# A hand-written instruction order replaced: step 0's queries are loaded first, W_in's four pieces in a row, and 118 steps sit on another engine

## The chip, the cores and the metric

The kernel runs on one NeuronCore of a Trainium2 chip. The core has TensorE (PE, matmuls and transposes into PSUM), VectorE (DVE), ScalarE (ACT), GpSimd (POOL) and SyncE (SP, which here only issues DMAs). Each engine works through its own instructions strictly in the order in which they were written, and waits at an instruction until everything that it reads or overwrites is ready. The metric is the time of one launch on the device, in microseconds (us). The kernel before takes 145.53 us, the median of three runs (145.13 to 146.61).

## The reference

A decayed linear attention (4 batches, 8 heads, 768 positions, head size 64, blocks of 64) is followed by a gated MLP with a spatial mixing matrix over the 768 positions. Inputs and output are float32.

```python
for b in range(nb):                                  # attention, block by block
    intra = einsum('bhic,bhjc->bhij', qb, kb) * Dmask
    intra = einsum('bhij,bhjd->bhid', intra, vb)
    inter = einsum('bhid,bhde->bhie', qb * lam_pow, kv_state)
    out[:, :, sl] = intra + inter
    kv_state = lam_block * kv_state + einsum('bhsd,bhse->bhde', kb * rev_pow, vb)
...
h = maximum(x @ w_in, 0); u, v = split(h)             # 512 -> 1024, halves of 512
v_n = (v - mean(v)) / sqrt(var(v) + 1e-06)
v_s = einsum('ts,bsd->btd', w_spatial, v_n) + b_spatial
return (u * v_s) @ w_out
```

## The kernel before, in words

Each batch of 768 positions is cut into three steps of 256, so the program has steps n = 0 to 11; batch b owns steps 3b to 3b+2. Attention and the first matrix product go step by step. The spatial mixing needs all three steps of a batch and so comes once a batch, and the output product follows it.

The whole order of the work is a string, ORDER, of 719 tokens such as `PV.0.1.6.T`. A token names a step of the work, its arguments (for most: the step or batch, a half or a part, at the end the PSUM bank or banks) and the engine: T is PE, D is DVE, A is ACT, P is POOL, S a DMA on SP's queue. The kernel emits the tokens from first to last under a manual schedule, so that each engine's instruction stream is the subsequence of its own letters. Data dependences, and the reuse of a buffer or of a bank, become semaphore waits. Eight PSUM banks exist, of which bank 7 holds the running state.

The steps that the text speaks of, with the lines of the profile:

- Loads (L196): LK.n, LQ.n, LV.n bring a step's keys, queries and values, 512 KB each, into three buffers per kind (n mod 3). WH.0 to WH.3 (L253) bring W_in in four pieces of 512 KB: 0 and 1 hold the v columns, 2 and 3 the u columns. WQ.0 to WQ.5 (L274) bring 128 rows each of W_spatial; WQ.0 and WQ.1 land where WH.0 and WH.1 were, WQ.4 and WQ.5 where WH.2 and WH.3 were, WQ.2 and WQ.3 in a place of their own. WP (L283) brings W_out, 1 MB.
- Casts to bf16 (L181 on ACT, L183 on DVE, L185 on POOL): CW.0 to CW.3 for W_in's v columns (512 elements a partition), CX.0 and CX.1 for its u columns (1024), WC.a for W_spatial (768), WX.0 and WX.1 for W_out (1024), VC.n or the halves VD.n for the values.
- Attention: KM and QM (L331) scale keys and queries by powers of lambda; TK and TQ (L366) transpose them on PE and EK and EQ copy them out of PSUM, in steps 0 to 6, where steps 7 to 11 use DMA transposes instead, DK (L344) and DQ (L348). SC (L396) makes the scores, MK (L401) masks them on DVE, KP (L425) adds to the state, SX, SY and SA (L440) copy the state out, AV (L459 for the state's part, L468 for the values) forms the output in two halves, EX (L486, shown at L181 or L183) puts it into SBUF as x transposed. FN is a read of one element that orders AV's two halves.
- MLP: PV (L493) makes v for 128 positions, EV (L498 on ACT, L500 on DVE) applies the maximum, BN (L508, L509) takes mean and variance, RA, RD and RB (L513, L518, L523) turn them into scale and shift, VN (L529 on ACT, L532 on DVE) normalizes. PU (L544) makes half of u for a step and EU (L498, L500) evicts it.
- Mixing: WT (L556) transposes W_spatial on PE and EW copies it out. GP (shown at L181 or L183) writes the bias into a bank, PW (L570, six matmuls of 384 columns) adds the mixing to it, GM (L576) multiplies by u. The last two matmuls of every PW read the normalized v of the third step of its batch, so that no PW ends before the last VN of its batch.
- Output: PO (L581) and PH (L590), EO and EH (copies), ST and SH (stores).
- Fillers: FL (L309) multiplies a tile of ones into a bank that nobody reads. There are 32 such matmuls, in both versions.

Of the kernel before, what the change touches and what calls it, by code (L numbers as in the profile page):

```python
# [36 lines left out]
GM.0.1.0.5.D GM.0.2.0.6.D WT.2.1.3.T WT.0.1.1.T EW.0.1.1.D WP.S VC.3.D EW.2.1.3.A GP.0.1.1.6.A PW.0.3.0.2.T
WT.1.1.4.T LK.5.S GM.0.3.0.2.D SC.3.1.0.1.T KP.3.5.T SC.3.0.2.3.T MK.3.1.0.1.D EW.1.1.4.A PW.0.1.1.6.T TK.4.2.0.T
MK.3.0.2.3.D GP.0.3.1.1.A GP.0.2.1.2.A SY.3.5.A PW.0.3.1.1.T SA.3.1.D SX.3.D GM.0.1.1.6.D GP.0.0.1.3.A TQ.4.2.4.T
PW.0.2.1.2.T GM.0.2.1.2.D GM.0.3.1.1.D PW.0.0.1.3.T GM.0.0.1.3.D EK.4.2.0.A EQ.4.2.4.A KM.5.0.P KM.5.1.P  # L40
AV.3.0.5.6.T SC.4.0.1.2.T KP.4.0.T FN.3.5.6.A AV.3.1.5.6.T SY.4.0.D SC.4.1.3.4.T EX.3.1.6.A TQ.5.2.0.T WX.0.A WX.1.A
EX.3.0.5.D MK.4.0.1.2.D SA.4.1.D MK.4.1.3.4.D SA.4.0.D LV.5.S PV.3.1.6.T PU.3.1.5.T PO.0.1.1.T PO.0.3.2.T TK.5.2.4.T
PV.3.0.3.T LV.6.S LK.6.S EK.5.2.4.D EO.0.1.1.A EQ.5.2.0.A EV.3.1.6.A EU.3.1.5.A EO.0.3.2.D VC.5.P AV.4.0.6.0.T
KP.5.6.T SC.5.0.1.2.T EV.3.0.3.A FN.4.6.0.D SC.5.1.4.5.T AV.4.1.6.0.T PU.3.0.3.T VC.6.P SA.5.0.D MK.5.1.4.5.D
MK.5.0.1.2.D KM.6.0.P KM.6.1.P LK.7.S LQ.7.S LQ.6.S KM.7.1.P QM.7.0.P QM.6.0.P QM.6.1.P EX.4.1.0.A EX.4.0.6.A
PV.4.1.0.T PV.4.0.4.T AV.5.0.1.5.T BN.3.1.D FN.5.1.5.D KP.6.2.T AV.5.1.1.5.T EV.4.0.4.A PO.0.2.4.T PO.0.0.6.T
# [597 lines left out]
```

## Time and profile before

| what | value |
|---|---|
| median of three runs | 145.53 us (145.13 to 146.61) |
| the profiled execution's own time | 144.71 us |
| its span, first to last instruction | 143.0 us |
| mean granted PE clock | 0.972 of full speed |
| busy: PE, DVE, ACT, POOL | 94%, 81%, 58%, 36% of the span |
| read from and written to HBM | 24.38 MB and 6.29 MB |

The span is the part that the trace shows; 1.7 us of the execution's own time lie around it. The 40-slice view has one digit for each 3.6 us: a 9 is an engine that is busy throughout. The busy time of PE contains the time in which a matmul waits in the array's pipeline, so that a full digit does not by itself mean full speed; the chain of waits tells which of its pieces released the next. In the rows of that chain the columns are the start in us, the length in us, and engine, tile, line and count.

### The profile page before, as it was taken

How to read it: one execution, taken by the hardware profiler on the slowest of the kernel's cores; microseconds unless marked ns; L12 is line 12 of the kernel's file. 1: busy time of each engine (PE TensorE's matmuls, PEld its weight loads, DVE VectorE, ACT ScalarE, POOL GpSimd, SP SyncE). 2: the span in 40 equal slices, each digit the busy share in tenths (PEclk: the TensorE clock that was granted, in tenths of full speed). 3: DMA queues.
4: the chain of work that ended last, by engine and by line, in shares of the span. 5: the costliest groups of instructions: out<-in, count | busy, mean ns of one | idle time of the engine just before them, and what ended most of it. 6: DMA issues, size and time to landing. Idle time of an engine off the chain costs nothing.

```text
span 143.0 us, 4741 instructions
## 1 busy us (share of the span) xinstructions
PE 133.8 (94%) x1999; PEld 87.7 (61%) x2014; DVE 115.3 (81%) x236; ACT 82.8 (58%) x158; POOL 51.9 (36%) x61
## 2 busy tenths in 40 slices
PE   5969999899999899999999999999999999999990
PEld 4448774676666667567666565676665665666630
DVE  3399798989997769699399988995798889874760
ACT  3422895798978577569611586689113627791121
POOL 5077710555095343991770006920822000000000
PEclk9975899999999999999999999999999999999998
DMA  3999999899999899959904799998994403930284
GB/s 87 347 347 346 386 323 315 294 339 313 337 302 344 259 288 324 285 166 290 293 0 78 49 282 354 180 142 238 276 257 126 177 5 117 406 139 0 78 324 185
DMA packets 54617, 33.60 MB, mean 235 GB/s; under 512 B 11715, under 2 KB 49859, under 8 KB 54596
## 3 DMA queue, kind: packets, MB, share of 16 engines
q1 hardware_dynamic: 54448, 33.17, 80.7%
q8 instruction: 15, 0.25, 0.7%
q10 hardware_dynamic: 148, 0.13, 0.3%
q14 instruction: 6, 0.05, 0.1%
HBM read 24.38 MB, written 6.29 MB: 215 GB/s over the span
## 4 chain that ended last, share of the span: by engine, by line
PE 83%; DVE 9%; ACT 3%; issue 2%; DVEq 0%; ACTq 0%
PE ps L570 21%; PE ps L581 14%; PE ps L493 13%; PE ps L544 11%; PE ps L396 5%; PE ps L366 5%; PE ps L309 4%; PE ps L468 4%; PE ps L425 3%; PE ps L459 2%; DVE st L508 2%; DVE qc L331 2%; DVE kc L331 2%; DVE vn L532 1%; DVE win_sb L183 1%
## 5 line engine op out<-in xcount | busy, mean ns | idle before, releaser
L570 PE MATMUL ps<-wt_sb,vn 128*128 128x384 bf16 x192 | 33.7, 326 | 0.5 <-ACT vn L529 0.3
L331 POOL TENSOR_TENSOR kc<-k_in,lv 128x512 bf16<-128x512 f32 x20 | 20.5, 1043 | 30.0 <-PE ps L493 11.5
L401 DVE TENSOR_TENSOR a_sb<-ps,m 128x1024 bf16<-128x1024 f32 x24 | 28.4, 1211 | 0.7 <-PE ps L425 0.6
L570 PEld LDWEIGHTS <-vn 128*128 128x128 bf16 x192 | 18.3, 98 | 12.3 <-ACT vn L529 0.6
L544 PE MATMUL ps<-xT,win_sb 128*128 128x256 bf16 x192 | 23.6, 273 | 0.5 <-DVE win_sb L183 0.5
L331 POOL TENSOR_TENSOR qc<-q_in,lqn 128x512 bf16<-128x512 f32 x18 | 19.3, 1090 | 10.2 <-DMA q_in<-in_q_dram 5.2
L493 PE MATMUL ps<-win_sb,xT 128*128 128x512 bf16 x89 | 22.3, 379 | 0.4
L581 PE MATMUL ps<-wout_sb,gT 128*128 128x512 bf16 x84 | 22.1, 379 | 0.4
L576 DVE TENSOR_TENSOR gT<-ps,uT 128x384 bf16<-128x384 f32 x32 | 16.8, 551 | 7.1 <-PE ps L570 6.7
L544 PEld LDWEIGHTS <-win_sb 128*128 128x128 bf16 x192 | 18.4, 98 | 5.1 <-DVE win_sb L183 0.7
L181 ACT ACTIVATE ps<-bsp 128x384 f32<-128x384 f32 x23 | 11.2, 490 | 10.7 <-DVE gT L576 6.7
L508 DVE BATCH_NORM_STATS2 st<-vh 128x6 f32<-128x512 bf16 x24 | 16.2, 676 | 1.1 <-ACT vh L498 1.1
L181 ACT ACTIVATE o_sb<-ps 128x512 f32<-128x512 f32 (+1 forms) x14 | 8.0, 579 | 15.4 <-PE ps L581 14.6
L493 PEld LDWEIGHTS <-xT 128*128 128x128 bf16 x96 | 8.8, 98 | 9.6 <-ACT xT L181 0.8
L498 ACT ACTIVATE vh<-ps 128x512 bf16<-128x512 f32 x20 | 11.7, 600 | 4.9 <-PE ps L493 3.2
L181 ACT ACTIVATE xT<-ps 128x512 bf16<-128x512 f32 x20 | 11.0, 598 | 5.8 <-PE ps L468 5.7
L581 PEld LDWEIGHTS <-gT 128*128 128x128 bf16 x92 | 8.7, 98 | 8.6
L498 ACT ACTIVATE uT<-ps 128x512 bf16<-128x512 f32 x20 | 11.7, 590 | 2.0 <-PE ps L544 2.0
L468 PE MATMUL ps<-a_sb,vb 64*64 64x128 bf16 x384 | 10.2, 220 | 0.3 <-issue 0.3
L396 PE MATMUL ps<-qT,kT 64*64 64x128 bf16 x384 | 9.7, 226 | 0.0
L309 PE MATMUL ps<-ones 128*128 128x256 bf16 x32 | 7.5, 368 | 1.6 <-DVE ones L305 1.5
L185 POOL CAST vb<-v_in 128x1024 bf16<-128x1024 f32 (+1 forms) x6 | 5.8, 965 | 7.8 <-PE ps L468 7.8
(79 smaller groups left out, 175.1 us busy)
## 6 DMA issues: line engine op xcount, KB each, us to landing
k_in<-in_k_dram SPq DMA_DIRECT2D x12, 512.0 KB, 6.4
q_in<-in_q_dram SPq DMA_DIRECT2D x12, 512.0 KB, 5.9
v_in<-in_v_dram SPq DMA_DIRECT2D x12, 512.0 KB, 6.1
out_dram<-o_sb SPq DMA_DIRECT2D x23, 256.0 KB, 2.5
wst<-in_moe_w_in_dram SPq DMA_DIRECT2D x4, 512.0 KB, 7.8
wst<-in_moe_w_spatial_dram SPq DMA_DIRECT2D x4, 384.0 KB, 4.5
wst<-in_moe_w_out_dram SPq DMA_DIRECT2D x1, 1024.0 KB, 8.9
wss<-in_moe_w_spatial_dram SPq DMA_DIRECT2D x2, 384.0 KB, 7.7
```

The lines of the kernel that those rows point to most:

```text
L181: nc.scalar.activation(out=o, in_=i, func=AF.Copy)
L331: vec(e).tensor_tensor(out=dst[n % NCA][:, u].rearrange("p u m o d -> p o (u m) d"), in0=src[n % NIN].rearrange("p (o u) m d -> p o u m d" ...
L396: nc.tensor.matmul(out=pa[o][row(c), w, j], lhsT=kT[n % NTR][row(o), u, j, c * Q64:(c + 1) * Q64], rhs=qv(n, o, u, c), start=(w == 0 and j ...
L401: nc.vector.tensor_tensor(out=a_sb[n % NA][:, i].rearrange("p o w j x -> p o w (j x)"), in0=ps[:, b0:b1 + 1:b1 - b0].rearrange("p o (w y) ...
L468: nc.tensor.matmul(out=po[c ^ o][row(w), c, i], lhsT=vb[n % NCA][row(c), 4 * o + u, j, :], rhs=a[row(c), i, o, w, j, :], start=(r == 0 and ...
L493: nc.tensor.matmul(out=bank(b), lhsT=x[:, slot(c, g)], rhs=win_sb[:, g, DH:DFF], start=(g == 0), stop=(g == NCH - 1))
L498: nc.scalar.activation(out=o, in_=i, func=AF.Relu)
L508: nc.vector.bn_stats(out=st6[p2][:, t], in_=vh[p2][:, t])
L544: nc.tensor.matmul(out=pu[:, f2].rearrange("p (c x) -> p c x", c=2), lhsT=win_sb[:, g, f * P:(f + 1) * P], rhs=x[:, slot(0, g):slot(1, g) ...
L570: nc.tensor.matmul(out=bank(b)[:, 0:HW], lhsT=vn[bb % 2][:, s, f * P:(f + 1) * P], rhs=wt_sb[:, s, i * HW:(i + 1) * HW], start=False, stop ...
L576: nc.vector.tensor_tensor(out=gT[bb % 2][:, f, cols], in0=bank(b)[:, 0:HW], in1=uT[bb % 2][:, f, cols], op=ALU.mult)
L581: nc.tensor.matmul(out=bank(b), lhsT=gT[bb % 2][:, f, t * P:(t + 1) * P], rhs=wout_sb[:, f, :], start=(f == 0), stop=(f == NCH - 1))
```

## The change

Nothing but the string ORDER is changed. The two strings hold the same 719 steps (the same 32 fillers among them); they stand in another order, many use other PSUM banks, and 118 of them name another engine. On each engine:

- Moved between engines, counted over the program: EO eight from ACT to DVE and seven back; EU six from ACT to DVE and three back; EV six and three; GP four and seven; VN two from ACT to DVE and five back; EX two and four; QM six from DVE to POOL and six back; KM two and four; VC three from ACT to POOL, two from POOL to ACT, one from DVE to ACT.
- In the part of batch 0 alone: CW.0 and CW.1 go from ACT to POOL, CW.2 from POOL and CW.3 from ACT to DVE; CX.0 from POOL and CX.1 from DVE to ACT; WC.0 and WC.1 from POOL to DVE, WC.3 from DVE and WC.4 from ACT to POOL, WC.5 from DVE to ACT; both QM.3 from DVE to POOL; EW.0.0 and EW.2.0 from ACT to DVE and EW.1.0 from DVE to ACT; EV.2.0 and EU.0.1 from ACT to DVE; EU.1.0, GP.0.2.0 and VC.3 from DVE to ACT; WX.0 from ACT to POOL and WX.1 from ACT to DVE.
- SP's queue, first part. Before: K0 Q0 Q1 K1 V0 Q2 K2 V1 WH.0 WH.1 V2 Q3 WH.3 WQ.0 WQ.1 WQ.2 WH.2 K3 K4 WQ.3 WQ.4 WQ.5 V3 Q4 Q5 V4 WP K5 V5. After: Q0 K0 K1 V0 Q1 K2 Q2 V1 WH.0 WH.1 WH.2 WH.3 V2 WQ.2 WQ.1 WQ.0 K3 WQ.3 WQ.4 WQ.5 Q3 V3 Q4 K4 V4 WP Q5 K5 V5.
- PE, first part: 24 of the 32 fillers stand ahead of the first transpose (14 before); the six PV and six PU of batch 0 and the first half of W_spatial's transposes come ahead of the first PW in both versions. TQ.3 stands ahead of the first PW before, TK.3 in its place after. The first two bias writes, GP.0.2.0 and GP.0.3.0, stand in ACT's stream ahead of the evictions of step 2; before, the first ones stand behind the last EU and VN of batch 0.
- Later: the four PU that separate the last PV of batch 2 from its first PW are 8.0, 6.1, 8.1 and 6.0, with no PO between them (before: three PU, PO.1.1 and PU.8.0).

The diff, cut to the lines of the first 37 us and to one place in each of batches 0 and 2 further on:

```diff
-LK.0.S LQ.0.S LQ.1.S LK.1.S LV.0.S LQ.2.S BR.A lam.A tab.0.A msk.P idn.P posk.P one.D row.D FL.2.256.0.1.T
...
-LV.1.S WH.0.S WH.1.S LV.2.S LQ.3.S WH.3.S VD.1.1.P CW.2.P EQ.1.0.1.D SX.0.D EQ.1.1.5.A SY.0.2.A EK.1.1.3.A
...
-EK.2.0.3.A SC.2.1.4.5.T FL.1.256.6.1.T CW.0.A CW.1.A SC.2.0.2.3.T AV.1.1.0.1.T WQ.0.S WQ.1.S WQ.2.S WH.2.S WC.0.P
-WC.1.P WC.2.P MK.2.1.4.5.D MK.2.0.2.3.D SA.1.1.D VC.2.D CW.3.A EX.1.1.1.A EX.1.0.0.A PV.0.1.6.T PV.0.0.4.T
-PV.1.0.5.T KP.2.6.T AV.2.0.2.3.T SA.2.0.D EV.0.1.6.A FN.2.2.3.A EV.0.0.4.A GP.0.0.0.1.A PV.1.1.6.T FL.1.256.0.1.T
-AV.2.1.2.3.T EX.2.0.2.A QM.3.1.D QM.3.0.D TQ.3.2.4.T CX.1.D PU.0.1.0.T PU.1.1.2.T EX.2.1.3.A EV.1.1.6.A BN.0.0.D
-EV.1.0.5.A BN.0.1.D RA.0.A EU.0.1.0.A EU.1.1.2.A PV.2.0.3.T PV.2.1.6.T BN.1.1.D BN.1.0.D EV.2.0.3.A RA.1.A
-EV.2.1.6.A WT.0.0.3.T WT.2.0.5.T EW.2.0.5.A PU.2.1.2.T WT.1.0.0.T BN.2.0.D RD.1.D BN.2.1.D VN.1.1.D RD.0.D RB.0.D
-EW.0.0.3.A RA.2.A VN.0.0.A CX.0.P PU.2.0.6.T EU.2.0.6.A VN.0.1.A EW.1.0.0.D RD.2.D LK.3.S PU.1.0.5.T PU.0.0.3.T
-VN.2.0.D VN.1.0.D VN.2.1.D LK.4.S WQ.3.S EU.1.0.5.D GP.0.2.0.6.D EU.2.1.2.A GP.0.1.0.5.A EU.0.0.3.A GP.0.3.0.2.A
...
-PU.8.1.3.T PU.6.1.4.T PU.7.0.5.T EV.8.0.2.A EU.8.1.3.A GP.2.2.0.2.A EU.6.1.4.A RA.7.A BN.8.1.D RD.6.D BN.8.0.D
...
+LQ.0.S LK.0.S LK.1.S LV.0.S LQ.1.S LK.2.S LQ.2.S LV.1.S WH.0.S WH.1.S BR.A lam.A tab.0.A posk.P idn.P msk.P one.D
...
+LN.3.A mkc.D LL.D BE.1.5.D eps.D LX.A KM.0.0.D KM.0.1.D FL.2.256.1.1.T FL.2.256.2.1.T FL.2.256.4.1.T FL.2.256.2.1.T
+FL.4.256.4.1.T FL.2.256.5.1.T QM.0.0.P FL.2.256.1.1.T TQ.0.0.0.T QM.0.1.P TK.0.1.6.T TK.0.0.3.T TQ.0.1.5.T
...
+AV.0.1.5.4.T TK.2.0.6.T FL.2.256.2.1.T FL.2.256.3.1.T TQ.2.1.2.T VD.1.1.A EX.0.0.5.A QM.2.0.P WH.2.S WH.3.S LV.2.S
+MK.1.1.0.1.D EQ.2.1.2.D FL.1.256.3.1.T KP.1.3.T AV.1.0.5.0.T TQ.2.0.1.T CW.0.P CW.1.P EX.0.1.4.A FN.1.5.0.A
+EK.2.0.6.A SA.1.0.D SY.1.3.D EQ.2.0.1.D AV.1.1.5.0.T SC.2.1.3.4.T EX.1.0.5.A EX.1.1.0.A SC.2.0.1.2.T SA.1.1.D CW.2.D
+CW.3.D PV.0.1.6.T EV.0.1.6.A CX.0.A PV.0.0.5.T PV.1.1.0.T PV.1.0.6.T EV.0.0.5.A PU.1.0.5.T MK.2.1.3.4.D BN.0.1.D
+MK.2.0.1.2.D BN.0.0.D WQ.2.S WC.2.P CX.1.A EV.1.1.0.A VC.2.D PU.0.1.2.T AV.2.0.3.4.T KP.2.6.T WQ.1.S WQ.0.S LK.3.S
+WQ.3.S WQ.4.S WQ.5.S LQ.3.S LV.3.S LQ.4.S PU.1.1.1.T KM.3.0.P KM.3.1.P WC.3.P WC.4.P GP.0.2.0.0.A EU.1.0.5.A RA.0.A
+EV.1.0.6.A GP.0.3.0.5.A FN.2.3.4.A BN.1.1.D SA.2.0.D BN.1.0.D RA.1.A RD.0.D WC.1.D RD.1.D VN.1.1.D WC.0.D RB.0.D
+VN.1.0.D EU.0.1.2.D AV.2.1.3.4.T EX.2.1.4.A EX.2.0.3.A PU.0.0.6.T PV.2.1.4.T WT.2.0.3.T EW.2.0.3.D EU.1.1.1.A
+EU.0.0.6.A EV.2.1.4.A BN.2.1.D WT.0.0.1.T PV.2.0.6.T WT.1.0.2.T PU.2.0.4.T VN.0.0.A VN.0.1.A EW.1.0.2.A EV.2.0.6.D
+BN.2.0.D PU.2.1.6.T TK.3.2.3.T EW.0.0.1.D EU.2.0.4.A RA.2.A GP.0.1.0.4.A EU.2.1.6.A WC.5.A GP.0.0.0.6.A EK.3.2.3.A
+RD.2.D VN.2.0.D VN.2.1.D PW.0.2.0.0.T PW.0.3.0.5.T WT.0.1.2.T WT.2.1.1.T PW.0.0.0.6.T LK.4.S EW.0.1.2.D GM.0.2.0.0.D
...
+SC.4.0.2.3.T AV.3.1.4.1.T EX.3.0.4.A WX.1.D PO.0.3.0.T EX.3.1.1.A PV.3.0.4.T EV.3.0.4.A KM.5.0.P MK.4.1.5.6.D
...
+RD.6.D RB.6.D VN.6.1.D BN.7.0.D EU.7.1.2.A EU.7.0.3.A EV.8.1.5.A VN.6.0.A EV.8.0.0.D BN.8.0.D BN.8.1.D PU.8.0.4.T
+PU.6.1.2.T RA.7.A RD.7.D RB.7.D GP.2.3.1.1.A RA.8.A RD.8.D VN.7.0.A VN.7.1.D RB.8.D VN.8.0.D VN.8.1.A PU.8.1.3.T
+QM.9.1.D EU.8.1.3.D PU.6.0.5.T PW.2.2.1.6.T PW.2.3.1.1.T EU.8.0.4.A GP.2.2.0.0.A GP.2.1.0.3.A PW.2.2.0.0.T
+PW.2.1.0.3.T ST.1.1.S DQ.9.S QM.10.1.P DQ.10.S DK.10.S ST.0.1.S GM.2.2.1.6.D GP.2.1.1.4.A GM.2.3.1.1.D GP.2.3.0.6.D
...
```

More of the change, by code (lines that the diff above doesn't have):

```diff
@@ L37 @@
[L37 to L46, printed above, removed]
@@ L85 @@
+GM.3.3.0.0.D GM.3.2.1.3.D GP.3.2.0.5.D GP.3.3.1.1.A PW.3.1.1.6.T GM.3.1.1.6.D PW.3.3.1.1.T GM.3.3.1.1.D PW.3.2.0.5.T
+GM.3.0.0.2.D ST.2.1.S GM.3.2.0.5.D ST.2.2.S ST.1.3.S ST.1.0.S ST.2.3.S ST.2.4.S ST.1.2.S ST.2.5.S ST.2.0.S
+PO.3.3.4.T PH.3.5.1.0.T EO.3.3.4.D PO.3.0.2.T PH.3.5.0.3.T PO.3.4.6.T PO.3.2.1.T EO.3.0.2.D EH.3.5.1.0.D
+EH.3.5.0.3.A SH.3.5.1.A PO.3.1.4.T EO.3.1.4.A ST.3.3.S ST.3.0.S SH.3.5.0.S EO.3.4.6.D ST.3.4.S EO.3.2.1.D ST.3.2.S
+ST.3.1.S
 """
```

91 lines of the change are left out of this document (44 added, 47 removed).

## Prediction

> **What bounds the kernel now.** I read the page first, for who is busy and when.
>
> ```profile
> span 143.0 us, 4741 instructions
> PE 133.8 (94%) x1999; PEld 87.7 (61%) x2014; DVE 115.3 (81%) x236; ACT 82.8 (58%) x158; POOL 51.9 (36%) x61
> PE   5969999899999899999999999999999999999990
> PEclk9975899999999999999999999999999999999998
> DMA  3999999899999899959904799998994403930284
> PE 83%; DVE 9%; ACT 3%; issue 2%; DVEq 0%; ACTq 0%
> ```
>
> PE is full and carries 83% of the chain that ended last. The other engines carry the rest, 12%, so the next question is where. The busy times by stage say where it is not:
>
> ```profile
> 19.82:35.12 15.30, 14.34 (x203) 9.96 (x205) 14.18 (x32) 12.10 (x26) 6.21 (x7) 1.00 0.97 312
> 36.36:49.59 13.23, 12.76 (x260) 9.22 (x261) 11.47 (x21) 9.92 (x17) 6.38 (x6) 1.00 1.01 309
> 50.00:137.00 87.00, 86.42 (x1230) 54.94 (x1240) 71.91 (x154) 49.19 (x98) 28.18 (x30) 1.00 0.73 190
> ```
>
> (The columns are the stage, its length, then busy time and count of PE, weight loads, DVE, ACT and POOL, the granted clock, DMA share and GB/s.) From 50 to 137 us PE idles 0.6 us of 87. Since both versions hold the same matmuls, no order can gain anything there; it can only lose. From 36.36 to 49.59 it idles 0.5 us. So whatever the new order gains, it gains ahead of 36.36 us. There the chain, in order of time, is not PE's:
>
> ```profile
> 20.51 1.18 PE ps L493 x5
> ...
> 23.96 1.28 DVE qc L331 x2
> 25.24 1.23 DVE win_sb L183
> ...
> 34.72 0.40 DVE vn L532
> 35.12 0.61 DVE uT L500
> 35.81 0.50 ACT ps L181
> 36.36 2.11 PE ps L570 x12
> ```
>
> The reader is to see a chain that leaves PE's first PV, runs through DVE's scaling of queries and a cast of W_in, ends with DVE's last normalization at 35.12, and then still takes an eviction of u and a bias write (ACT, ps) before the mixing product (L570) runs freely from 36.36. Six of its matmuls had been done by then. What PE could have done between is the sum of its pieces, priced from later places where PE is full (rows of the same chain; the AV rows are the state's part and the values' part of one half):
>
> ```profile
> 40.56 0.34 PE ps L556 x6
> 41.24 0.35 PE ps L425 x32
> 53.01 0.45 PE ps L366 x8
> 54.31 0.24 PE ps L459 x8
> 54.55 0.22 PE ps L468 x16
> 61.58 0.86 PE ps L493 x4
> 62.45 0.87 PE ps L544 x8
> 105.53 0.97 PE ps L570 x6
> ```
>
> From the first PV to the first PW both versions do six PV (5.16), six PU (5.22), two AV halves (0.92), one KP (0.35), three WT (1.02) and one transpose of step 3 (0.45): 13.1 us. With the 0.97 of the six early matmuls taken off, 36.36 is worth an undisturbed start of PW at 35.39. From 20.51 that is 14.9 us for 13.1 us of work: 1.8 us are there to be won, and not more.
>
> **The loads.** On SP's queue WH.2 and WH.3 pass V2 and Q3, and WH.2 the three WQ as well. These rows give issue and landing of V2 and WH.3 (start of the issue, then us to landing), and the uses that waited on WH.1 and WH.2:
>
> ```profile
> 12.80 0.47 SPq L196 DMA_DIRECT2D v_in<-in_v_dram  x1
> 15.26 4.00 SPq L253 DMA_DIRECT2D wst<-in_moe_w_in_dram  x1
> 19.39 0.61 POOL L185 CAST win_sb<-wst 128x512 bf16<-128x512 f32 x1 [1.50 <-DMA wst<-in_moe_w_in_dram]
> 22.41 0.67 DVE L183 CAST vb<-v_in 128x1024 bf16<-128x1024 f32 x1
> 29.86 1.04 POOL L185 CAST win_sb<-wst 128x1024 bf16<-128x1024 f32 x1 [0.56 <-DMA wst<-in_moe_w_in_dram]
> ```
> ```profile
> v_in<-in_v_dram SPq DMA_DIRECT2D x1, 512.0 KB, 7.9
> wst<-in_moe_w_in_dram SPq DMA_DIRECT2D x1, 512.0 KB, 8.4
> ```
>
> V2 lands at 20.7, WH.3 two places later at 23.7: 1.5 us a place on a DMA side that is full (digit 9). WH.1 has the tenth place in both orders, so CW and with it the first PV stay at 19.4 and about 20.3. WH.2 then lands at 20.7 instead of 29.86 and WH.3 at 22.2, so no PU waits for W_in any more. The price is V2, which goes from 20.7 to 23.7. VC.2 (0.67) then ends no earlier than 24.4. In the new order four PV and two PU (5.2 us from 20.3, so until 25.5) stand ahead of AV.2, which covers V2 by 1 us; DVE reaches VC.2 after two masks and two BN at about the same time. Behind V2, WQ.2, WQ.1 and WQ.0 (three quarters of a place each) land by 27.1. Q3 falls from 22.2 to about 34, some eight places on; its first use is TQ.3, behind three PW and two WT after the new start of PW, so at about 38, and POOL scales it in between. I cost the loads at nothing, and V2's cover at 1 us.
>
> **DVE up to the first PW.** DVE is busy 14.18 of the 15.30 us from its first mask of step 2 to the last VN, so its queue sets the end. The rows for what moves:
>
> ```profile
> L183 DVE CAST wsp_raw<-wst 128x768 bf16<-128x768 f32 x1 | 0.5, 547 | 0.0
> L183 DVE COPY wt_sb<-ps 128x768 bf16<-128x768 bf16 x2 | 1.1, 546 | 0.0
> L500 DVE TENSOR_SCALAR vh<-ps 128x512 bf16<-128x512 f32 x4 | 2.7, 681 | 0.0
> L440 DVE TENSOR_TENSOR s_sb<-ps,ysb 128x256 bf16<-128x256 f32 x16 | 6.4, 411 | 1.4 <-ACT ysb L181 0.9 <-PE ps L425 0.5
> ```
>
> Away go two QM.3 (1.28), CX.1 (1.31 in its own row, 1.23 on the chain) and SA.1.1 (0.41, now done before the weights land): 2.9 to 3.0. In come WC.0 and WC.1 (1.09), one more EW (0.55), EU.0.1 and EV.2.0 (0.68 each): 3.0, and CW.2 and CW.3. A DVE cast of 512 float32 elements is not in the trace; two thirds of the 768 row is 0.37, half of the 1024 row (1.31, with POOL beside it) 0.66. I take 0.45, nearer the row that ran undisturbed. DVE's work from 19.4 to the last VN is then 14.18 + 0.05 + 0.9 = 15.1 us, between 14.9 and 15.5. Its waits were 1.1 us before; the new order may have none or as many. So the last VN ends between 34.3 and 36.0. PW's sixth matmul follows it, and five of the six are done by then, so PW starts in effect 0.8 us earlier, at 33.5 to 35.2; PE's own work (20.3 + 13.1 = 33.4) does not bind. The bias writes no longer stand behind VN: GP.0.2.0 and GP.0.3.0 are written some 8 us ahead. Against 35.39 the gain is 0.2 to 1.9 us. I take the middle, 1.1: on DVE the new order saves no work at all, it gains only that nothing stands between the last VN and PW. ACT takes CX.0 and CX.1 in this stretch, which is what is late next: it was busy 12.10 of 15.30 us.
>
> **Ahead of the first PV.** Queries first and keys on DVE end where keys first ended, since WH.1 at 19.4 bounds what follows; casts on POOL, VC.0 and the keys' evictions on ACT have 2 us and more to spare. I cost this at nothing, if PE's clock allows (below).
>
> **After the first PW.** Each eviction that I followed has its cover, with two exceptions. EX.3.0 and EX.3.1 both go to ACT, where one of them was DVE's, with one PO (0.86) between AV.3 and PV.3:
>
> ```profile
> L181 ACT ACTIVATE xT<-ps 128x512 bf16<-128x512 f32 x20 | 11.0, 598 | 5.8 <-PE ps L468 5.7
> ```
> ```profile
> qT<-qc SPq DMA_TRANSPOSE x5, 4.2
> ```
>
> Two of them, 1.2, exceed the cover by 0.3. And batch 2's first PW has four PU (3.5 us) after the last PV where it had 4.3 us; the chain EV, BN, RA, VN behind that PV is 0.6 + 0.86 + 0.3 + 0.8 = 2.6 plus its queueing, on the edge. There QM.9.1, now on DVE, comes behind the batch's VN, about 4 us after the last PV; DQ.9 waits for it at the head of SP's queue, with DQ.10, DK.10 and ST.0.1 behind it, and lands 4.2 us after its issue (row above), at 8.2. SC.9 reads it after four PU and six PW, 3.5 + 5.8 = 9.3 us. Covered by 1 us. I put 0.4 us for all of this; bounds are -0.5 (the idle of 36.36 to 49.59 vanishes) and 2. The casts WX leave ACT for POOL and DVE and cost nothing, since W_out is loaded one place earlier.
>
> **Sum.** -1.1 + 0.4 = -0.7 us on the profiled execution: 144.0 of its 144.71, span 142.3. That execution lies 0.8 below the median of the runs, so the median is 145.53 - 0.7 = 144.8 us.
>
> **Rivals.** (1) More is won: DVE waits nowhere (-1.9) and the idle of 36 to 50 goes as well (-0.4): 143.2. For it: PE's work alone would allow 33.4. Against: ACT has new casts there.
> (2) Slower, by PE's clock. The 40-slice row of the clock has a 5 in the fourth slice, and by the single microsecond:
>
> ```profile
> 8.00:9.00 1.00, 0.52 (x9) 0.34 (x7) 1.00 (x2) 0.00 (x0) 1.00 (x2) 0.79 1.16 348
> 15.00:16.00 1.00, 1.00 (x48) 0.75 (x40) 0.79 (x3) 0.98 (x3) 0.70 (x1) 0.79 1.04 406
> ```
>
> After PE had been half idle the clock fell to 0.5, from about 8.8 to 15.2, 6.4 us, and it came back after five full microseconds. The new order spends 24 fillers before the first transpose and leaves 8 for what follows, where 18 were. If the half clock therefore begins later and lies on the first PV, 6.4 us at half speed do 3.2 us less work; 1.3 of it fits into the slack between 33.4 and the 34.7 that I took for PW, and 1.9 stays, or 2.3 with DVE waiting for the late v: 144.8 + 2.3 = 147.1. It decides once PE is still at 0.5 at 21 us. Against: the attention of steps 1 and 2 gives PE dense work from 13 us, whatever the fillers. The Trainium skill, TensorE: Matmul & The Clock Gate, section "What's actually happening", says that the clock halves after an idle window of about 3.4 us and returns after about as long a busy one, the window running freely. The trace's 6.4 us at half speed is two of these; by the rule alone a single cold window would cost 1.7 us less its slack, and the time would stay near 145.2.
> (3) No change: V2's 3 us come through, because DVE or ACT reaches step 2 a microsecond late, and eat the gain: 145.5 to 146.
>
> **Numbers.** Forecast 0.40 (its own range 144.1 to 145.4), rival 1 0.28, rival 2 0.24, rival 3 0.08. The range is 143.0 to 147.3: below it lies the lowest tenth, above it the clock rival's end. About 1% is what a measurement of this kernel can tell from no change, 144.07 to 146.99. Faster by over 1%: rival 1 without its edge, 0.27, and 0.02 of the forecast. Slower: rival 2, 0.24, and 0.01. Same: the rest, 0.46.
>
> **What would show it.** Right: WH.2's cast at about 21 to 22; AV.2 at 25 to 26; the last VN of batch 0 at 34.3 to 36.0 with a PW running beside it and no bias write in the chain there; PE's idle after 50 us below 1.5 us. Wrong: a granted clock of 0.5 past 20 us; AV.2 waiting for VC.2; DVE's EU or EV in that stretch waiting for ACT's casts; SC.9 behind a DMA wait; idle of PE in the batches 1 to 3.

## The result, and the profile after

| kernel | median of the runs | range | runs |
|---|---|---|---|
| before | 144.80 us | 143.48 to 146.61 | 20 |
| changed | 145.97 us | 144.86 to 147.11 | 20 |

The ratio is 1.011, with a 95% interval of 1.008 to 1.013: the changed kernel is slower by about 1.1%, where the prediction had it faster by 0.5% (144.8 of 145.53). Here and below a ratio is taken of the fast executions alone, those within 1.5% of the fastest of their kernel, and medians and ranges hold all of them. The profiled execution of the changed kernel took 146.46 us and its span is 144.0 us, 1.0 more than the span of before. First the page of the changed kernel: span, busy times, granted clock.

```profile
span 144.0 us, 4765 instructions
...
PE 134.4 (93%) x2014; PEld 86.6 (60%) x2014; DVE 120.4 (84%) x230; ACT 85.2 (59%) x164; POOL 53.9 (37%) x61
...
PEclk9999999999999999999999999999999999999999
```

The 9 in every slice says a full clock, but not for the start: the trace holds its first record of the granted clock at 9.07 us, and ahead of a first record the views print 1.00. The four transposes at 8.53 us take 0.63 us, where before's at 7.46, in a stretch recorded at full clock, take 0.40: up to 9.1 us this kernel runs at half clock, and from there on at full clock. In before the half clock lasts from 8.6 to 15.4. DVE is busy for 5.1 us more (115.3 before), with 230 instructions where it had 236. Next the busy times by stage, from the end of what precedes the first PV to the end of the last VN of batch 0, and from 50 us on (columns as in the prediction).

```profile
19.18:36.61 17.43, 14.95 (x174) 9.57 (x167) 16.47 (x32) 13.22 (x27) 6.83 (x7) 1.00 1.06 353
50.00:138.00 88.00, 87.79 (x1249) 55.62 (x1248) 77.53 (x156) 49.47 (x99) 25.53 (x26) 1.00 0.68 180
```

From 50 us on PE idles 0.2 us of 88, so nothing was lost there, as before. Ahead of it DVE works 16.47 of 17.43 us, and its last VN ends at 36.61 (before: 35.12). The chain of waits, in order of time, shows on which instructions:

```profile
19.26 3.70 PE ps L493 x16
...
27.77 1.24 DVE vn L532
29.01 1.31 DVE wsp_raw L183
30.32 0.63 DVE nmr L523
30.95 0.97 DVE vn L532
...
34.42 1.03 PE ps L544 x8
...
35.91 2.08 PE ps L570 x12
...
40.23 2.06 DVE qc L331 x2
...
42.86 0.50 ACT ps L181
...
43.41 1.14 PE ps L570 x6
```

The first PV starts at 19.26, 1.25 us earlier than before (20.51). PW then runs freely from 35.91, 0.5 us later than the 35.39 that before was worth. So the stretch between them takes 16.65 us where it took 14.88, for the same 13.1 us of PE's work. In the chain stand four instructions of DVE in a row, VN.1.1, WC.0, RB.0 and VN.1.0, with 4.15 us together, and the third of them makes two numbers for each partition. The chain then leaves DVE by EV.2.0, which frees the bank of the PU at 34.42; no row has PE waiting for the last VN itself, which stands in the same queue. The ledger against before is -1.25 + 1.77 + 0.48 = +1.0 us, the difference of the spans; the 0.48 behind PW's start is what remains of it. The largest wait there is 0.59 us at one place: the two QM.4 (L331, 2.06), the GM behind them, a bias write on ACT, and PE's group at 43.41 behind that. Before idled there too, 0.5 us between 36.36 and 49.59, so this wait is not by itself the 0.48. What ran beside these two places is seen in POOL's timeline (start, length, engine, line, operation, tiles, count; in brackets the idle time before and what ended it; the length of a row that groups several is their sum):

```profile
27.82 2.09 POOL L331 TENSOR_TENSOR kc<-k_in,lv 128x512 bf16<-128x512 f32 x2 [2.68 <-DVE rstd L518]
29.86 1.15 POOL L185 CAST wsp_raw<-wss 128x768 bf16<-128x768 f32 x1
30.95 0.82 POOL L185 CAST wsp_raw<-wst 128x768 bf16<-128x768 f32 x1
...
40.31 1.50 POOL L185 CAST vb<-v_in 128x1024 bf16<-128x1024 f32 x1
```

Two KM.3, WC.3 and WC.4 fill POOL without a pause from 27.82 to 31.77, which is where the four instructions of DVE stand, and VC.4 lies on the second QM.4.

### The profile page after: what moved, and what is told of

Its sections match the earlier page's. It is cut to its first block, busy times and chain, and to the rows that moved or that the text cites. A ratio compares the mean times of both kernels' runs of the same rounds, so it can differ in the third digit from the quotient of the medians.

```text
span 144.0 us, 4765 instructions
## 1 busy us (share of the span) xinstructions
PE 134.4 (93%) x2014; PEld 86.6 (60%) x2014; DVE 120.4 (84%) x230; ACT 85.2 (59%) x164; POOL 53.9 (37%) x61
## 4 chain that ended last, share of the span: by engine, by line
PE 73%; DVE 17%; DMA 5%; issue 1%; ACT 1%; SPq 0%; DVEq 0%; ACTq 0%
PE ps L570 21%; PE ps L544 13%; PE ps L493 12%; PE ps L581 11%; PE ps L396 4%; DMA k_in<-in_k_dram 3%; PE ps L468 3%; PE ps L366 3%; DVE kc L331 3%; DVE qc L331 2%; PE ps L459 2%; PE ps L425 2%; DVE a_sb L401 2%; DVE vn L532 2%; DMA out_dram<-o_sb 1%
## 5 line engine op out<-in xcount | busy, mean ns | idle before, releaser
L570 PE MATMUL ps<-wt_sb,vn 128*128 128x384 bf16 x192 | 33.1, 326 | 0.6 <-ACT ps L181 0.6
L331 POOL TENSOR_TENSOR kc<-k_in,lv 128x512 bf16<-128x512 f32 x18 | 19.8, 1116 | 30.5 <-DMA k_in<-in_k_dram 11.6
L581 PE MATMUL ps<-wout_sb,gT 128*128 128x512 bf16 x92 | 22.7, 380 | 0.0
L331 POOL TENSOR_TENSOR qc<-q_in,lqn 128x512 bf16<-128x512 f32 x18 | 19.5, 1095 | 7.9 <-ACT lqn L226 3.0
L181 ACT ACTIVATE ps<-bsp 128x384 f32<-128x384 f32 x26 | 12.3, 488 | 7.9 <-DVE a_sb L401 4.8
L181 ACT ACTIVATE xT<-ps 128x512 bf16<-128x512 f32 x22 | 12.2, 595 | 4.1 <-PE ps L468 3.9
L498 ACT ACTIVATE vh<-ps 128x512 bf16<-128x512 f32 x17 | 10.1, 596 | 7.0 <-PE ps L493 6.9
L185 POOL CAST vb<-v_in 128x1024 bf16<-128x1024 f32 (+1 forms) x7 | 7.4, 1058 | 10.1 <-ACT seen L181 5.5
L498 ACT ACTIVATE uT<-ps 128x512 bf16<-128x512 f32 x17 | 9.8, 589 | 0.6 <-PE ps L544 0.5
L183 DVE COPY o_sb<-ps 128x512 f32<-128x512 f32 (+1 forms) x12 | 7.9, 665 | 2.5 <-PE ps L581 2.4
L396 PE MATMUL ps<-qT,kT 64*64 64x128 bf16 x384 | 8.9, 219 | 1.0 <-DVE kT L183 0.8
```

What stands on the lines that cost most here:

```text
L181: nc.scalar.activation(out=o, in_=i, func=AF.Copy)
L331: vec(e).tensor_tensor(out=dst[n % NCA][:, u].rearrange("p u m o d -> p o (u m) d"), in0=src[n % NIN].rearrange("p (o u) m d -> p o u m d" ...
L396: nc.tensor.matmul(out=pa[o][row(c), w, j], lhsT=kT[n % NTR][row(o), u, j, c * Q64:(c + 1) * Q64], rhs=qv(n, o, u, c), start=(w == 0 and j ...
L498: nc.scalar.activation(out=o, in_=i, func=AF.Relu)
L570: nc.tensor.matmul(out=bank(b)[:, 0:HW], lhsT=vn[bb % 2][:, s, f * P:(f + 1) * P], rhs=wt_sb[:, s, i * HW:(i + 1) * HW], start=False, stop ...
L581: nc.tensor.matmul(out=bank(b), lhsT=gT[bb % 2][:, f, t * P:(t + 1) * P], rhs=wout_sb[:, f, :], start=(f == 0), stop=(f == NCH - 1))
```

## The experiments

My theory after these views: DVE's instructions that read and write SBUF are held up while a POOL instruction runs, and the new order puts the casts of W_spatial, the normalizations and QM.4 exactly there. The rivals: DVE's queue is merely longer by two casts; the late load of V2; the clock and the fillers. Ratios are to the kernel before, timed on the same chip; line numbers differ by one or a few where a kernel's order takes fewer or more lines.

### POOL's work of step 3 held back

```diff
-PU.1.1.1.T KM.3.0.P KM.3.1.P WC.3.P WC.4.P GP.0.2.0.0.A
+PU.1.1.1.T GP.0.2.0.0.A
...
-VN.1.0.D EU.0.1.2.D
+VN.1.0.D GN.1.0.P KM.3.0.P KM.3.1.P WC.3.P WC.4.P EU.0.1.2.D
...
-GM.0.0.0.6.D QM.3.1.P QM.3.0.P
+GM.0.0.0.6.D GN.2.1.P QM.3.1.P QM.3.0.P
```

GN.n.c is a copy on POOL of one element of the tile that VN.n.c writes, so that POOL waits there for that VN.

> The changed kernel with one edit: POOL's two products of k for step 3 and its casts of W_sp rows 3 and 4 are held back until VectorE's v_n 1.1 and 1.0 are done, and its products of q for step 3 until v_n 2.1 is done; every engine but POOL keeps its work and order. Theory (VectorE's instructions from SBUF to SBUF are stretched while a POOL instruction runs): v_n 1.1 falls from 1.24 to about 0.43 us, the cast of W_sp row 0 from 1.39 to about 0.55, the small product behind it from 0.77 to about 0.2, v_n 1.0 from 0.98 to about 0.43, 2.8 us of VectorE's queue in all; the first product with W_sp starts 1.5 to 2.5 us earlier, and the ratio to the kernel before falls from 1.011 to between 0.993 and 1.001. Rival (the queue is long because two casts more stand in it, whatever POOL does): the durations stay and so does the ratio, 1.011, or rises to 1.02 since POOL's work is late.

Measured: 143.95 us, ratio 0.995 (0.992 to 0.999). DVE's timeline of this kernel:

```profile
27.77 0.41 DVE L531 TENSOR_SCALAR vn<-vh,mv,rstd 128x512 bf16<-128x512 bf16 x1
28.10 0.55 DVE L182 CAST wsp_raw<-wst 128x768 bf16<-128x768 f32 x1
28.57 0.15 DVE L522 SCALAR_TENSOR_TENSOR nmr<-mv,rstd 128x2 f32<-128x2 f32 x1
28.64 0.41 DVE L531 TENSOR_SCALAR vn<-vh,mv,rstd 128x512 bf16<-128x512 bf16 x1
...
30.07 0.68 DVE L507 BATCH_NORM_STATS2 st<-vh 128x6 f32<-128x512 bf16 x1
```

POOL's timeline of it, with the two KM.3 that were held back:

```profile
29.25 2.03 POOL L330 TENSOR_TENSOR kc<-k_in,lv 128x512 bf16<-128x512 f32 x2
```

Its busy times from the same start to the end of the last VN:

```profile
19.18:33.79 14.61, 14.30 (x172) 9.63 (x167) 13.65 (x32) 12.88 (x27) 4.54 (x7) 1.00 1.08 367
```

And PE's timeline, with the PW that runs freely and the later group that waits:

```profile
33.05 2.11 PE L569 MATMUL ps<-wt_sb,vn 128*128 128x384 bf16 x12
...
40.95 1.14 PE L569 MATMUL ps<-wt_sb,vn 128*128 128x384 bf16 x6 [0.59 <-ACT ps L180]
```

The four instructions start at the same 27.77 and take 1.28 us in place of 4.15. The stage holds the same 32 instructions of DVE as in the changed kernel, with 13.65 us of work in place of 16.47: 2.8 us, with nothing changed on DVE. The row at 30.07 is a control: this BN, which reads SBUF once, lies on POOL's KM.3 and takes the 0.68 us that it takes everywhere. PW runs freely at 33.05, and the whole kernel gains 1.5% on the changed one. The rival of a merely longer queue is out. The second place is still there (0.59 at 40.95), as it should be.

### QM.4 back on POOL

```diff
-QM.4.0.D QM.4.1.D EW.2.1.1.A
+EW.2.1.1.A
...
-QM.3.0.P KM.4.0.P KM.4.1.P
+QM.3.0.P QM.4.0.P QM.4.1.P KM.4.0.P KM.4.1.P
```

> The changed kernel with one edit: the two products of q for step 4 go back from VectorE to POOL, ahead of step 4's products of k. Theory: the 2.13 us that they hold VectorE at 40.2 us beside POOL's cast of v is the whole of the stall at 42 to 43 us (the g product behind them, the bias write behind that, TensorE's group behind that), so TensorE gains 0.8 to 1.2 us there and the ratio to the kernel before falls from 1.011 to 1.003 to 1.006. Rival (this stall is covered by a later wait, or the 2 us more on POOL come back as a wait for k of step 4): 1.009 to 1.015.

Measured: 146.33 us, ratio 1.000 (0.996 to 1.004). Its twelve executions fall into two groups, four of 143.8 to 145.5 and eight of 146.2 to 147.0 us; the ratio is that of the four, and the profile is of the eight. By the medians of all executions it would be 1.011 (146.33 to 144.81), which is the rival's value: the numbers do not decide between the two. POOL's timeline in that profile:

```profile
35.53 2.25 POOL L330 TENSOR_TENSOR qc<-q_in,lqn 128x512 bf16<-128x512 f32 x2 [1.00 <-PE ps L365]
```

And its chain of waits, in order of time:

```profile
35.42 1.47 DVE vn L531 x2
...
36.94 1.31 PE ps L569 x7
```

The wait at 43 us is gone, as expected, but in this execution the QM.4 that POOL now starts at 35.53 falls on DVE's last two VN, which take 1.47 us for 0.73 in the changed kernel, and PE waits for them. The collision has moved to a place that bounds the stage just as much. That the faster group is the one that escapes it is not shown.

### The two casts of W_spatial back on POOL

```diff
-WC.1.D RD.1.D VN.1.1.D WC.0.D
+WC.1.P RD.1.D VN.1.1.D WC.0.P
```

> The changed kernel with one edit: the casts of W_sp rows 1 and 0 go from VectorE to POOL, at the places that they have in the order, so the one of row 0 behind step 3's products of k and the casts of rows 3 and 4. Theory (contention): VectorE loses 0.54 and 1.39 us of work, but v_n 1.1 and 1.0 and the small product keep their 0.4 to 0.8 us of excess each, and the transposes of W_sp get row 0 later, at about 32 to 33.5 us in place of 30.4: no gain, 1.008 to 1.025. Rival (VectorE's queue is merely two casts too long, 2 x 0.55 us): the first product with W_sp starts about 1.1 us earlier, 1.003.

Measured: 149.39 us, ratio 1.032 (1.028 to 1.037). In the order as it now stands they come behind POOL's KM.3, WC.3 and WC.4, and PE's timeline shows the price:

```profile
33.24 1.46 PE L555 MATMUL ps<-ident,wsp_raw 128*128 128x128 bf16 x12 [4.08 <-POOL wsp_raw L184]
```

That is four microseconds of wait for W_spatial; RB.0 and VN.1.0 beside POOL are still 1.00 and 1.21 us long. The direction is the theory's, the size is over its range, because WC.1 and WC.0 end at 33.2 and PE's first WT, with all that stands behind it in PE's queue, waits for them. "Undo the cast" is no test of the cast's cost when the queue that it returns to has changed as well.

### V2 loaded first

```diff
-WH.2.S WH.3.S LV.2.S
+LV.2.S WH.2.S WH.3.S
```

> The changed kernel with one edit: v of step 2 is loaded ahead of the two u halves of W_in instead of behind them, as in the kernel before. Theory (the order of the loads is not the cause): no gain, since v of step 2 is landed when its cast comes up in the queue; the u halves land some 1.5 us later and their casts on ScalarE with them, 1.010 to 1.020. Rival (the late load of v 2 costs time): 1.000 to 1.006.

Measured: 146.57 us, ratio 1.010 (1.007 to 1.014), the changed kernel's own. So V2's late load is not what loses the time. The u halves now come later and PE waits 0.61 us at 23.66 for ACT behind their casts; how this and other small differences add up to the same ratio was not taken apart.

### Both edits together

The first two diffs in one, with QM.4 on POOL behind the held-back QM.3.

> The changed kernel with the edits of the two runs before put together: POOL's products of k 3 and casts of W_sp 3 and 4 held back until v_n 1.0, its products of q 3 until v_n 2.1, and the products of q 4 on POOL behind these. Theory (contention, and 2.5 us of VectorE's queue at 37.4 us that no longer stand ahead of the g product): v_n of step 2 stays undisturbed, since POOL starts the products of q only behind it, and the wait of TensorE for the bias write (0.59 us at 40.4) goes: 0.6 to 1.2 us less than the 143.95 us of the first, a ratio of 0.987 to 0.991. Rival (POOL becomes late with k and v of step 4): 0.995 to 1.000.

Measured: 143.06 us, ratio 0.988 (0.984 to 0.992). It is faster than both kernels. PE's timeline from 19 to 58 us has one single row with an idle time ahead of it:

```profile
46.50 0.59 PE L580 MATMUL ps<-wout_sb,gT 128*128 128x512 bf16 x2 [0.34 <-DVE wout_sb L182]
```

That is 0.34 us of waiting in 39 us: behind the first PV PE is as full in batch 0 as it is after 50 us.

### The same cure for the kernel before

```diff
-KM.3.0.P WQ.4.S
+GN.2.1.P KM.3.0.P WQ.4.S
```

> The kernel before with one edit: POOL's first product of k for step 3 is held back until v_n 2.1 is done. Theory (contention is in the kernel before too): the small product at 32.16 us falls from 0.81 to 0.15 us, the three v_n at 33.54 from 1.58 to 1.2 us, the first product with W_sp starts 0.8 to 1.1 us earlier, and the ratio is 0.993 to 0.997. Rival (another wait bounds this stage in the kernel before): 0.999 to 1.003.

Measured: 145.35 us, ratio 1.003 (0.999 to 1.007): a miss. Three rows of DVE's timeline in the kernel before:

```profile
32.16 0.81 DVE L523 SCALAR_TENSOR_TENSOR nmr<-mv,rstd 128x2 f32<-128x2 f32 x1
...
33.54 1.58 DVE L532 TENSOR_SCALAR vn<-vh,mv,rstd 128x512 bf16<-128x512 bf16 x3
...
36.10 1.28 DVE L331 TENSOR_TENSOR kc<-k_in,lv 128x512 bf16<-128x512 f32 x2
```

The same three with the edit:

```profile
32.25 0.16 DVE L522 SCALAR_TENSOR_TENSOR nmr<-mv,rstd 128x2 f32<-128x2 f32 x1
...
32.98 1.06 DVE L531 TENSOR_SCALAR vn<-vh,mv,rstd 128x512 bf16<-128x512 bf16 x3
...
35.02 2.26 DVE L330 TENSOR_TENSOR kc<-k_in,lv 128x512 bf16<-128x512 f32 x2
```

And the row of PE's timeline with the edit that waits longest there:

```profile
38.74 0.73 PE L555 MATMUL ps<-ident,wsp_raw 128*128 128x128 bf16 x10 [0.50 <-DVE wsp_raw L182]
```

The first half of the expectation holds: RB.0 falls from 0.81 to 0.16, the three VN from 1.58 to 1.06, 1.2 us together. But POOL's KM.3.0, and KM.4.0 behind it, now lie on the two KM that DVE makes next, which take 2.26 in place of 1.28 us; the cast of W_spatial behind them is late and PE waits for it. The stage wins and the next one pays. The kernel before had the same collision, and holding POOL back does not by itself remove it.

### W_in's casts where they were

```diff
-CW.0.P CW.1.P EX.0.1.4.A FN.1.5.0.A EK.2.0.6.A
+CW.2.P EX.0.1.4.A FN.1.5.0.A EK.2.0.6.A CW.0.A CW.1.A
...
-EX.1.1.0.A SC.2.0.1.2.T SA.1.1.D CW.2.D CW.3.D
+EX.1.1.0.A CW.3.A SC.2.0.1.2.T SA.1.1.D
```

> The changed kernel with one edit: the four casts of W_in's v half go back to where the kernel before has them, one on POOL and three on ScalarE. If the casts' new place is why the first product with W_in starts at 19.2 us instead of 20.4: it starts at 20.0 to 20.6 us again, and the ratio is 1.011 to 1.019. If the order and clock of TensorE ahead of it are why: it starts at 19.2 to 19.6 us, VectorE is rid of 0.7 us, and the ratio is 1.006 to 1.011.

Measured: 146.35 us, ratio 1.013 (1.007 to 1.019). PE's timeline at the first PV:

```profile
19.19 1.18 PE L492 MATMUL ps<-win_sb,xT 128*128 128x512 bf16 x3
21.19 1.02 PE L492 MATMUL ps<-win_sb,xT 128*128 128x512 bf16 x4 [0.82 <-ACT win_sb L180]
```

It starts at 19.19 as in the changed kernel, so the casts are not why it starts early; but it then waits 0.82 us for ACT's cast, and PW runs freely at 36.25, 0.4 us later than with the casts on POOL and DVE. The ratio lies just above the 1.006 to 1.011 that was expected, and the difference of 0.2% to the changed kernel lies within the intervals: what moving these casts is worth to the whole kernel is not shown.

### More fillers in the kernel before

```diff
-TQ.0.0.3.T FL.2.256.1.1.T
+FL.2.256.1.1.T TQ.0.0.3.T FL.2.256.1.1.T
...
-TQ.0.1.4.T TK.0.1.5.T
+TQ.0.1.4.T FL.4.256.1.1.T TK.0.1.5.T
```

> The kernel before with one edit: six more filler matmuls in TensorE's two idle times at 6.8 and 8.5 us, which should keep its granted clock at 1.0 where it fell to 0.5 from 8.8 to 15.2 us. If the half clock is why its first product with W_in starts at 20.4 us: this starts 0.5 to 1.2 us earlier. The time then falls (0.993 to 0.998) only if the VectorE queue behind it moves with it; with VectorE and POOL as they are the ratio is 0.998 to 1.002, which is the theory here. Rival: the clock does not hold or is not what limits, the first product stays at 20.4 us, 1.000.

Measured: 144.43 us against 144.98 for the kernel before, ratio 0.989 (0.983 to 0.996), with single times between 142.4 and 145.6 us. The busy times by stage of this kernel (the clock is the third number from the end):

```profile
12.00:14.00 2.00, 1.84 (x64) 1.41 (x62) 2.00 (x3) 0.45 (x1) 1.52 (x2) 1.00 1.15 348
```

PE's timeline of it at the first PV:

```profile
19.46 2.83 PE L492 MATMUL ps<-win_sb,xT 128*128 128x512 bf16 x12
```

The half clock does not vanish, but it lasts 3.4 us (8.4 to 11.8) where it lasted 6.8 (8.6 to 15.4), and the first PV starts at 19.46 in place of 20.44 us (in PE's timeline; the chain of waits prints 20.51). That fits the half clock as what held the kernel before there, but the run does not isolate it: DVE's KM at 7.93 takes 0.69 us here where it took 1.55 in before, which helps the same transposes. The last run below comes back to this. How much of that microsecond reaches the end stays open: the ratio of 0.989, beyond what either side expected, rests on three of its six executions (142.4 to 144.3, the first of them the profiled one), and by the medians of all it is 0.996.

### Five copies that nobody waits for

```diff
+    def x_p(e):
+        nc.gpsimd.tensor_copy(out=dummy, in_=bsp)
...
-WC.2.P CX.1.A
+WC.2.P XP.P XP.P XP.P XP.P XP.P CX.1.A
```

> The combined kernel of the run before, with five copies added on POOL that nobody waits for: the bias tile (128x768, 32 bits) to a scratch tile in bf16, from 25.3 us on behind the cast of W_sp row 2, some 0.83 us each, which ends at about 29.4 us where POOL was idle. Theory (contention): VectorE's casts of W_sp rows 1 and 0, its two v_n of step 1 and the three tiny instructions among them are longer by 0.4 to 0.85 us each, 2 to 3 us together; its statistics and its readings of PSUM keep their times; the first product with W_sp starts 1.5 to 3 us later and the ratio rises from 0.988 to 0.998 to 1.009. Rival (a POOL instruction that nobody waits for costs nothing): 0.986 to 0.990.

Measured: 143.64 us, ratio 0.994 (0.991 to 0.998), 0.6% over the combined kernel that it was made from. It lies between the two expected ranges, and the two intervals overlap by a hair, so the effect on the whole kernel is not clear of the noise; the rows decide. DVE's timeline of this kernel:

```profile
27.17 1.04 DVE L183 CAST wsp_raw<-wst 128x768 bf16<-128x768 f32 x1
...
28.31 0.72 DVE L535 TENSOR_SCALAR vn<-vh,mv,rstd 128x512 bf16<-128x512 bf16 x1
...
29.42 0.77 DVE L526 SCALAR_TENSOR_TENSOR nmr<-mv,rstd 128x2 f32<-128x2 f32 x1
```

POOL's timeline of it, with the five copies in one row:

```profile
25.18 5.00 POOL L210 CAST dummy<-bsp 128x768 bf16<-128x768 f32 x5
```

WC.1 is 0.50 longer than in the combined kernel, VN.1.1 0.31, RB.0 0.61; WC.0 and VN.1.0 slip through. That is 1.4 us, and the last VN ends 1.5 us later (35.23, was 33.70). Work that nobody waits for, on an engine with nothing else to do, lengthens three instructions of another engine: this is the cause shown by putting it back. The size is half of what I expected, and why only three of the instructions were hit is not shown. POOL lost as well: five copies take 5.00 us, where W_spatial's casts of the same shape take 0.82 each when they have their way.

### No fillers ahead of the first transposes

```diff
-LX.A KM.0.0.D KM.0.1.D FL.2.256.1.1.T FL.2.256.2.1.T FL.2.256.4.1.T FL.2.256.2.1.T
-FL.4.256.4.1.T FL.2.256.5.1.T QM.0.0.P FL.2.256.1.1.T TQ.0.0.0.T
+LX.A KM.0.0.D KM.0.1.D QM.0.0.P TQ.0.0.0.T
```

> The changed kernel without the sixteen filler matmuls that stand between the decay tables and the first transposes (their sums are never read). If the fillers keep TensorE's clock, and the clock is why the first product with W_in starts at 19.2 us: the granted clock falls to about 0.5 for some 6 us from about 8 us on, and the product starts 0.6 to 1.3 us later, at 19.8 to 20.5 us. The time then rises by no more than that, 1.011 to 1.020, and by less if VectorE's queue behind it is what sets the first product with W_sp. Rival: the clock stays at 1.0 without them, the product starts at 19.2 us, 1.011.

Measured: 145.07 us, ratio 1.004 (1.001 to 1.007), which is below the changed kernel's interval. PE's timeline has the first eight transposes of keys:

```profile
9.12 1.03 PE L364 MATMUL ps<-ident,kc 128*128 128x128 bf16 x8 [1.39 <-DVE kc L329]
```

The same eight in the changed kernel:

```profile
9.12 0.62 PE L366 MATMUL ps<-ident,kc 128*128 128x128 bf16 x8
```

PE's timeline at the first PV without the fillers:

```profile
19.44 3.63 PE L491 MATMUL ps<-win_sb,xT 128*128 128x512 bf16 x16
```

DVE's timeline of it:

```profile
27.42 0.41 DVE L530 TENSOR_SCALAR vn<-vh,mv,rstd 128x512 bf16<-128x512 bf16 x1
...
28.22 1.00 DVE L521 SCALAR_TENSOR_TENSOR nmr<-mv,rstd 128x2 f32<-128x2 f32 x1
29.14 1.21 DVE L530 TENSOR_SCALAR vn<-vh,mv,rstd 128x512 bf16<-128x512 bf16 x1
```

The view prints a clock of 1.00 from 8 to 10 us here too, but the trace's first record of it is at 12.26 us, and the eight transposes take 1.03 us where the changed kernel has 0.62: without these fillers PE runs at half clock for 3 us longer. Nine profiles with the changed kernel's fillers have the first record of full clock between 7.8 and 10.9 us, the two without them at 12.3 and 15.1. So the fillers do bring the full clock earlier, and yet the first PV moves by 0.25 us only. The rows of DVE show where the kernel gains on the changed one: its queue is 0.35 us earlier, VN.1.1 runs at 27.42 before POOL starts its KM.3 at 27.87, and WC.0 behind it takes 0.55 as well. Only RB.0 and VN.1.0 are hit, 1.65 us in place of 2.87. In this one profile a third of a microsecond decides which instructions collide.

### A smaller dose, and the combined kernel without fillers

The first has the first diff with GN.1.1 in place of GN.1.0, put behind VN.1.1, and without GN.2.1; the second is the combined kernel with the diff of the run before.

> The changed kernel with POOL's products of k 3 and casts of W_sp 3 and 4 held back only until the first v_n (1.1) of VectorE is done, some 0.5 us, as a smaller dose of the first run. Theory (contention): v_n 1.1 at 0.41 us and the cast of W_sp row 0 at 0.55 us are undisturbed, the small product (about 1.0 us) and v_n 1.0 (about 1.2 us) are not: an excess of 1.7 us in place of 2.8, so 1.1 us of the 2.0 to 2.3 us that the first run won, a ratio of 1.001 to 1.006. The run without fillers has the same two instructions undisturbed, since its VectorE queue is 0.35 us earlier and POOL's start is not, and gave 1.004. Rival (that run's gain comes from the sixteen matmuls less): 1.010 to 1.013 here.

> The combined kernel (POOL's work held back and the products of q 4 on POOL) without the sixteen filler matmuls. Theory (the run without fillers won by the phase of the collision alone): with the collisions away there is nothing more to win, 0.985 to 0.991. Rival (the sixteen matmuls themselves cost 0.7% in the changed kernel): 0.980 to 0.983.

Measured: the smaller dose 147.47 us, ratio 1.015 (1.009 to 1.021); the combined kernel without fillers 142.86 us, ratio 0.987 (0.982 to 0.992). The second says what it was to say: with the collisions away the fillers are worth nothing that can be measured, so the rival that they cost 0.7% by themselves is out. Its trace, whose first record of full clock is at 15.1 us, also shows what a half clock up to there does. Two rows of PE's timeline of it:

```profile
13.43 1.03 PE L364 MATMUL ps<-ident,qc 128*128 128x128 bf16 x8
...
20.66 3.63 PE L491 MATMUL ps<-win_sb,xT 128*128 128x512 bf16 x15
```

Up to 11.9 us PE's rows are those of the kernel of the run before, which had the full clock from 12.3 on and its first PV at 19.44. Here the half clock lasts 2.8 us longer and the first PV starts at 20.66, 1.2 us later and close to the 20.44 of the kernel before, whose half clock ended at 15.4. So it is the half clock up to 15 us that puts the first PV there. At the end little of it is left: the span is 141.6 us, where the combined kernel with its full clock from 8.0 us has 141.3.

The smaller dose is a miss on the far side, for which 1.001 to 1.006 was expected; the profile is of the slowest of its six executions (148.88 us, the others 146.35 to 148.72). DVE's timeline in it, the row of RB.0:

```profile
28.58 3.67 DVE L522 SCALAR_TENSOR_TENSOR nmr<-mv,rstd 128x2 f32<-128x2 f32 x1
```

POOL's timeline of it beside that row:

```profile
28.67 2.03 POOL L330 TENSOR_TENSOR kc<-k_in,lv 128x512 bf16<-128x512 f32 x2
30.66 0.81 POOL L184 CAST wsp_raw<-wss 128x768 bf16<-128x768 f32 x1
31.42 0.82 POOL L184 CAST wsp_raw<-wst 128x768 bf16<-128x768 f32 x1
```

VN.1.1 and WC.0 escape, as meant. But RB.0, which takes 0.15 us alone, starts 0.09 us ahead of POOL's KM.3 and is done only when POOL's four instructions, which follow each other without a pause, have ended, at 32.2: 3.67 us. VN.1.0 behind it falls on QM.3 (1.22), PE stands still for 3.4 us and its granted clock drops to 0.72 between 34 and 38 us. In the changed kernel the same four POOL instructions let DVE in between each two: the four instructions of DVE end at 29.01, 30.32, 31.02 and 31.92, each 0.0 to 0.4 us behind the end of one of POOL's. So the excess is not a sum over instructions that can be read off beforehand; what decides whether DVE gets in between stays open, and so does what RB.0 takes in the five executions without a profile.

## Why the prediction was wrong, point by point

**What bounds the kernel: right.** Nothing was lost or won from 50 us on; all of the +1.0 us arises ahead of it.

**The loads: right.** W_in's u casts run on ACT at 20.90 and behind, VC.2 at 23.79 and AV.2 directly behind PU at 25.2, with no wait for V2. With V2 loaded first the ratio is no better (1.010). Rival 3 had neither its cause nor its time.

**Ahead of the first PV: wrong, by 1.25 us to the good.** "WH.1 at 19.4 bounds what follows" did not hold: PE needs the four casts one after another, and starts on the first. What held the kernel before there was in the main its half clock: the first PV starts at 20.44 with it until 15.4 us, at 20.66 in the kernel without fillers that has it until 15.1, and at 19.44 in the one that has it until 12.3. The prediction had seen the half clock, which by the trace lasts 6.8 us (8.6 to 15.4) and not 6.4, since a microsecond at 0.79 has 0.42 us at half; but it asked only whether the new order would get a worse one (rival 2), not what the old one cost. The changed kernel has no half clock behind 9.1 us, so rival 2 is false. Its sum also set the slack against a PW at 34.7, where the forecast's own gain of 1.1 puts it at 34.3; nothing hangs on that now.

**DVE up to the first PW: this is the step that failed.** The sum "14.18 + 0.05 + 0.9 = 15.1 us, between 14.9 and 15.5" was 16.47 on the chip, and the last VN, put at 34.3 to 36.0, ended at 36.61 although the stage began 1.25 us earlier. The instructions are those of the sum and the waits (0.96 us) lie in its bounds; the durations do not hold. WC.0 was taken at 0.55 and had 1.39, and the VN, RB and WC of step 1 have 2.87 us of excess together beside POOL's work, which disappear when POOL is held back (13.65 us). The prediction saw such a pair in the trace of before (a cast of 1.31 "with POOL beside it") and used it to choose a mean, not as a price that depends on what POOL does at that moment; and it never laid POOL's new queue (both QM.3, WC.3 and WC.4 added) beside DVE's. The sum was even too large for an undisturbed DVE, as its base of 14.18 held the old collisions, RB.0 at 0.81 and three VN at 1.58, which are 1.2 us.

**After the first PW: +0.4 forecast, +0.5 measured, and the agreement is luck.** The 0.4 was put down to evictions, batch 2 and a transpose; the wait that the trace shows is at another place. EX.3, batch 2's edge and DQ.9 cost nothing that shows; QM.4, which moved to DVE beside VC.4, was not priced.

**The sum.** -0.7 became +1.0 in the span of the profiled executions, +1.2 in the medians of twenty. The forecast time of 144.8 us is that of the kernel before in twenty runs (144.80), by chance: the median of three on which it was built, 145.53, was 0.7 too high. With POOL held back the ratio is 0.995, which is the forecast's, but by other terms, so that this agreement is luck too: PW 2.3 us earlier than before, not 1.1, and 1.2 us given back after it, of which the combined kernel recovers 0.6.

On the cause, the rows first: casts and scalings from SBUF to SBUF, and products with two inputs in SBUF, are longer beside POOL by 0.3 to 0.9 us, in one case by 3.5; the readings of PSUM and BN are not. The Trainium skill, SBUF — State Buffer, section "Who interferes with whom", says that DVE shares one of its pairs of SBUF ports with GpSimd, that the one which issues first has the pair for the whole of its instruction and the other blocks until it is done, and it names copies, casts, tensor_scalar and instructions with two inputs in SBUF as those that can contend. The trace agrees on which instructions are hit; a wait for one instruction alone is not what the 3.67 us behind four of them show, in one profile. The port itself is in no trace here: shown is that POOL's activity is the cause.

## What to carry to other kernels

When a step moves between DVE and POOL, or merely in time, lay the two queues beside each other and give every SBUF-to-SBUF instruction of DVE two prices, alone and beside POOL; a POOL instruction that nobody waits for can still set the end. Put POOL's work beside DVE's readings of PSUM and its statistics, and tie it there with a dependence rather than by hope, since a third of a microsecond decides; then check what it lies on next, as the kernel before gained nothing from being cured in one place only. An early resource that is visibly slow (a half clock) should be priced for the old kernel too, not only for the new; and where a view prints a full clock at the start of a trace, compare the length of a matmul there with the same one later.
